# Regrouping the scores to three and five, one signed feature block per projection, and other places for 44 early units, in a two-branch attention kernel

## Chip, cores and metric

One core of one Trainium2 chip. The metric is the device time of one launch in microseconds (us); the time of a kernel is the median over its runs. Engines are named as in the profile: PE (TensorE), PEld (its weight loads), DVE (VectorE), ACT (ScalarE), POOL (GpSimd), SP (SyncE, which issues the DMAs).

## The reference

Inputs: x of 2048 tokens by 448, two sets of projection weights, a per-head feature matrix and a gate vector; 16 heads of 28.

```python
def _A_ref(x, wqkv, w_phi, wo):                   # linear attention with learned features
    q, k, v = ...                                 # x @ wqkv, by heads
    pq, pk = q @ w_phi, k @ w_phi                 # per head
    phi_q = concat([softmax(pq), softmax(-pq)])   # phi_k likewise from pk
    kv, z = phi_k^T v, sum(phi_k)
    return ((phi_q kv) / (phi_q z + 1e-6)) @ wo
def _B_ref(x, wqkv, wo):                          # full softmax attention
    return (softmax(q k^T * 28**-0.5) v) @ wo
g = sigmoid((x * gate_w).sum(-1))
return g * a + (1 - g) * b
```

The features of branch A need, for each head and token, the largest value and the smallest value of 28 numbers before two exponentials, exp(p - max) and exp(min - p).

## The kernel before, in words

The order of work on PE, DVE, ACT and POOL is the order of the Python calls (`manual_schedule`); only the DMAs on SP are placed by the framework. Times below are of the profiled execution.

**Projection of q and k of branch B** (to about 65 us): for n = 4 to 19 `proj_qk` (line 577) runs 11 matmuls into one PSUM bank, ACT and DVE split the result into a high and a low part (`keep_qk`, line 586) and SP writes it to DRAM. Weights are split in the same way by `split_weight` (line 141): a cast on ACT (line 143), a difference on DVE or POOL (line 144). `wvA` is split at n = 16 and 18 (line 688).

**Units** (`mx_unit`, line 259): the exact row maximum of the scores of branch B, which the softmax subtracts, costs a second pass over q k^T. In the early part it is done in 44 units: four matmuls on 28 rows side by side into two double banks `pmb` and `pmd` (line 285), a Relu of `pmd` on ACT (line 288), two add-and-max operations on DVE (line 290). There are two double-buffered banks for `pmb` and `pmd`, so a unit waits until DVE and ACT have read the one before. The units are sprinkled over the early loops by hand (lines 685, 733, 772, 818, and `tick`, line 719, inside a projection).

**Branch A** (about 65 to 316 us), the loop at line 727 over i = 0 to 42, with t = i for the keys (t < 16) and q = i - 16 for the queries. For each tile of 128 tokens `features1` (line 438) copies the projected block from PSUM to `pc` on ACT (line 441), takes maximum and minimum over each head on DVE (lines 443, 444), and makes the two differences (lines 447, 449: the first on POOL, the second on POOL or, for q = 1 to 8, on DVE). The exponential follows on ACT (line 452) one iteration later, and `features2` (line 455) sums on DVE, inverts, and multiplies on POOL (line 461). Features go to one of four buffers, `feats`. Keys end in `kv_add` (line 473); queries go through `turn` (transposes, copied to `fT` on ACT, line 528), `numer` (copied to `oUa` on ACT, line 399), a normalisation through DRAM, and `out_a` (line 557). At q = 2 the PSUM pool is closed and a new one opened with four single banks in place of three and the bank of `pkv`. From q = 18 the values of branch B are projected (`value_b`, line 712); `wvB` is split at q = 14 and 17.

**Branch B** (from about 332 us), the loop at line 1139 over s = 0 to 255. A step s is one tile of 128 keys against a block of 4 heads and 512 queries; 16 steps make a block, and there are 16 blocks. `scores` (line 879) does four matmuls `st` of 128x512 into four PSUM banks (line 885) and four exponentials on ACT (line 903); `values(s - 1)` does four column-tiled matmuls `pv` (line 1017) on the exponentials of the step before; `mx_visit` (line 305) carries on the row maxima: four row-tiled matmuls `pm` (line 322) into four more banks, one Relu or copy on ACT (line 326), two or three maxima on DVE (line 333) and mostly one add-and-max on DVE (line 330). PE thus runs st x4, pv, pm, st x4, and so on. Seven banks are dealt out from a list, `free`, by `scores` and `mx_banks` (line 956); an eighth holds the sum of `pv`. In the steady state the four banks of a step's `st` are, in order: the third and the fourth of the step before, the last one that DVE read of the `pm` of two steps before, and the one that ACT's Relu read of the `pm` just before. From s = 191 scores come in groups of eight, one for two steps, and a visit in every other step. `project` (line 1022) and the tail use the same list.

Of the kernel before, what the change touches and what calls it, by code (L numbers as in the profile page):

```python
# [17 lines left out]
P = 128  # L18
# [22 lines left out]
def gated_mix_kernel(ctx, tc, xT, wqkB, wvB, wvA, wkAT, wqAT, phi, woA, woB,  # L41
# [17 lines left out]

    psn = [3, 2]  # L60

    def ps_s(nm):
        return ps.tile([P, 512], F32, tag="s", name=nm, bufs=psn[0])

    def ps_pv(nm):
# [371 lines left out]

    def features1(pp, nm, eng):

        pc = bd.tile([P, H, DH], F32, tag="pc", name=f"pc{nm}", bufs=2)  # L440
        nc.scalar.copy(pc, pp[:, :D].rearrange("p (h f) -> p h f", f=DH))
        ext = bd.tile([P, 2, H], F32, tag="ext", name=f"ext{nm}", bufs=3)
        nc.vector.tensor_reduce(ext[:, 0, :], pc, AX.X, ALU.max)
        nc.vector.tensor_reduce(ext[:, 1, :], pc, AX.X, ALU.min)
        f = feats[feats_used[0] % 4]
        feats_used[0] += 1
        nc.gpsimd.tensor_sub(f[:, :, :DH], pc,
                             ext[:, 0, :].unsqueeze(2).to_broadcast([P, H, DH]))
        eng.tensor_sub(f[:, :, DH:2 * DH],
                       ext[:, 1, :].unsqueeze(2).to_broadcast([P, H, DH]), pc)  # L450
        fx = f[:, :, :2 * DH]
        exps.append(lambda: nc.scalar.activation(fx, fx, AF.Exp))
        return f
# [158 lines left out]
    def split_part(w, key, n, i, low=nc.vector):  # L612
        split_weight(w, raws[key][i], slice(2 * i, 2 * i + 2), slice(0, n), low)

    def splits(n):

# [47 lines left out]
    for n in range(4, NP):  # L664
        take_acts()
        if n in (4, 5):
            x_loads(n - 2)
        if n == 8:
            nc.sync.dma_start(phi_s, phi)
            load_fold(wkAT, "k")  # L670
        if n == 10:
            part_loads("wB1", wqkB[:, :, 512:896], 384, "wB1")
        splits(n + 1)
        if n == 14:
            part_loads("wvA", wvA, 450, "wvA")
            nc.sync.dma_start(sel_s, sel)
            nc.sync.dma_start(mask_s, mask)
            for v in vap:
                nc.gpsimd.memset(v[:, :, 28:32], 0.0)
                nc.gpsimd.memset(v[:, :, 28:29], 1.0)  # L680
            feats = [bd.tile([P, H, 64], F32, name=f"feat{i}") for i in range(4)]
            for f in feats:
                nc.gpsimd.memset(f[:, :, 56:], 0.0)
        if 16 <= n < 20:
            mx_unit()
        proj_qk(n, ev)
        if n in (16, 18):
# [39 lines left out]
    for i in range(2 * NT + 11):  # L727
# [14 lines left out]
        if q == 2:  # L742
            bk_s.close()
            ta_s = ExitStack()
            ta = ta_s.enter_context(tc.tile_pool(name="ta", bufs=1, reuse_waits="tile"))
            stg = ta_s.enter_context(tc.tile_pool(name="stg", bufs=2, reuse_waits="tile"))
            KV = ta.tile([P, 512], F32, name="KV")
            kvT = kv_copy()
            ps_s_.close()
            ps = ps_s_.enter_context(tc.tile_pool(name="psq", bufs=1, space=PSUM, reuse_waits="tile"))  # L750
            psn[0] = 4
            woA_s = weights(3, "woA_s")
            wvB_s = weights(2, "wvB_s")
            take_exps()
# [124 lines left out]
    def scores(s, i):  # L879
# [8 lines left out]
        if s == 0:  # L888
# [6 lines left out]
            return  # L895
        sts = []
        for j in (2 * i, 2 * i + 1):
            used.append(free.pop(0))
            sts.append(bank(used[-1], f"st{s}_{j}"))
            score(j, sts[-1])  # L900
        for j, st in enumerate(sts, 2 * i):
            p = p_slot(f"p{s}_{j}")
            nc.scalar.activation(p, st, AF.Exp, scale=SCALE)  # L903
            pts.setdefault(s, []).append(p)
        if i == 1:
            a, m = used[:], held[:]
            if s < TWO:
                free.extend([a[0], m[0], a[1], m[1], a[2], a[3], m[2]] if m else a)
            elif s % 2:
                free.extend([m[0], a[0], m[1], a[1]] if m else a)  # L910
                rest.extend([m[2], a[2], a[3]] if m else [])
            else:
                free.extend(rest + a)
                rest.clear()
            used.clear()
            held.clear()

    qst = [stack("qst0", False)]
    kst = [stack(f"kst{i}", True) for i in range(5)]
# [4 lines left out]
    ps_s_.close()  # L924
    ps = ps_s_.enter_context(tc.tile_pool(name="psv", bufs=1, space=PSUM, reuse_waits="tile"))
    psn[:] = 2, 3
    rlp = fr_s.enter_context(tc.tile_pool(name="rlp", bufs=1, reuse_waits="tile"))
    mx_unit()
    rest = NF - mxs["u"]
# [17 lines left out]

    free, used, held = list(range(7)), [], []  # L950
    spare, rest = [], []

    def bank(i, nm):
        return ps2.tile([P, 512], F32, tag=f"g{i}", name=nm, bufs=1)

    def mx_banks(f, first):
        b = [free.pop(0) for _ in range(4)]
        free.append(b[0])
        held.extend(b[1:])
# [62 lines left out]
    def project(qb, oT, tl):  # L1022
# [1 line left out]
        t = qb * 4 + tl  # L1024
        acc = acc_of[qb][:, tl, :]
        b = free.pop(0)
        free.append(held.pop(0) if held else b)
        if free[-1] != b:
            held.insert(0, b)
# [109 lines left out]
    for s in range(NS + 16):  # L1139
        take_acts()  # L1140
        if s < NS:
# [105 lines left out]
```

## Time and profile before

| | |
|---|---|
| time, median of 3 runs | 1017.42 us (1017.32 to 1019.32) |
| time of the profiled execution | 1015.89 us |
| its span on the core | 1014.1 us |
| instructions | 17989 |
| PE busy | 1002.8 us (99%) |
| ACT busy | 815.7 us (80%) |
| DVE busy | 679.7 us (67%) |
| POOL busy | 236.0 us (23%) |
| granted PE clock | 1.00 throughout |

The profile is of one execution. An engine is busy while one of its instructions runs; for PE the end of a matmul is modelled, and pipelined matmuls overlap, so that a PE that is busy all the time may still run under its best pace. Where an engine was idle before an instruction, the profile names the instruction that ended last among those it waited for. In the rows a time in us and a length in us stand first, then the engine, the line, the operation, the tile written and those read, the shape and a count of merged instructions; what stands in square brackets is the idle time before and what ended it.

### The profile page before, as it was taken

What the parts mean: (1) busy time and instruction counts of PE and PEld (TensorE: products, weight loads), DVE (VectorE), ACT (ScalarE), POOL (GpSimd) and SP (SyncE); (2) the same over time, 40 slices, a digit from 0 to 9 for tenths busy, and PEclk for the clock granted to TensorE, in tenths of its full rate; (3) what the DMA queues carried; (4) which work ended last, traced back from release to release, by engine and by line L of the source; (5) the groups of instructions that cost most, each with busy time, mean ns of one, the idle gap of its engine ahead of it and who ended that gap; (6) DMA issues with size and microseconds to landing.
All of it is one profiled execution on the core that took longest, in us unless ns stands there. A gap on an engine that the chain in (4) does not pass through costs nothing.

```text
span 1014.1 us, 17989 instructions
## 1 busy us (share of the span) xinstructions
PE 1002.8 (99%) x6472; PEld 561.9 (55%) x6472; DVE 679.7 (67%) x1340; ACT 815.7 (80%) x1534; POOL 236.0 (23%) x213
## 2 busy tenths in 40 slices
PE   9999999999999999999999999999999999999998
PEld 8878888868779433343333334333333344454656
DVE  6466666997753578888887888788888874544202
ACT  5445445678762899999999999999999999979682
POOL 1235456588435102111011110101201011001010
PEclk9999999999999999999999999999999999999999
DMA  8973110132245703233622223522323345615131
GB/s 295 311 241 93 60 50 3 44 90 83 93 129 128 155 20 84 64 73 69 128 65 70 55 58 79 127 65 55 87 56 76 75 101 155 157 34 150 57 109 55
DMA packets 64250, 98.89 MB, mean 98 GB/s; under 512 B 18176, under 2 KB 24944, under 8 KB 64160
## 3 DMA queue, kind: packets, MB, share of 16 engines
q1 hardware_dynamic: 64160, 97.74, 35.9%
q8 instruction: 51, 0.84, 0.4%
q14 instruction: 39, 0.32, 0.1%
HBM read 69.54 MB, written 27.78 MB: 96 GB/s over the span
## 4 chain that ended last, share of the span: by engine, by line
PE 90%; DVE 5%; DMA 2%; ACT 1%; POOL 1%; issue 1%; SPq 0%; DVEq 0%; POOLq 0%; ACTq 0%
PE st L885 29%; PE pv L1017 25%; PE pm L322 9%; PE pk L127 4%; PE pva L127 4%; PE poa L109 4%; PE pqk L109 3%; PE pob L109 3%; PE pvb L109 2%; PE pvb L127 2%; PE pq L109 2%; DMA qkd<-ev 1%; PE pmb L285 1%; PE pqk L652 1%; DVE fsumq L459 1%; DVE rl L290 1%
## 5 line engine op out<-in xcount | busy, mean ns | idle before, releaser
L903 ACT ACTIVATE p<-st 128x512 f32<-128x512 f32 x1020 | 522.4, 619 | 25.9 <-PE st L885 25.8
L333 DVE TENSOR_REDUCE part<-pm 128x1 f32<-128x512 f32 x477 | 304.6, 685 | 150.3 <-PE pm L322 144.3
L885 PE MATMUL st<-qst,kst 128*128 128x512 f32 x1024 | 309.8, 429 | 0.9 <-ACT vb L715 0.5
L1017 PE MATMUL pv<-p,vb 128*32 128x512 f32 x2048 | 266.1, 603 | 0.0
L885 PEld LDWEIGHTS st<-qst,kst 128*128 128x128 f32 x1024 | 174.2, 187 | 120.0 <-issue 52.4
L322 PEld LDWEIGHTS pm<-kc,qc 28*128 28x128 f32 x848 | 40.5, 181 | 177.8 <-ACT p L903 150.9
L326 ACT ACTIVATE rl<-pm 128x512 f32<-128x512 f32 x212 | 126.9, 598 | 10.8 <-PE pm L322 0.7
L420 POOL TENSOR_TENSOR oUb<-oUb,rsb 128x512 f32<-128x512 f32 x15 | 19.3, 1289 | 462.3 <-DMA rsb<-rdb 328.9
L330 DVE CUSTOM_DVE_ANT_0 rl<-pm,rl 128x512 f32<-128x512 f32 x159 | 108.1, 680 | 0.0
L322 PE MATMUL pm<-kc,qc 28*128 28x512 f32 x848 | 106.8, 495 | 0.0
L1017 PEld LDWEIGHTS pv<-p,vb 128*32 128x32 f32 x2048 | 45.5, 108 | 73.6 <-issue 67.4
L290 DVE CUSTOM_DVE_ANT_0 rl<-pmb,rl 128x512 f32<-128x512 f32 x88 | 57.0, 685 | 29.4 <-ACT rl L288 29.4
L109 PE MATMUL pqk<-XH,wB 128*128 128x512 f32 x192 | 59.3, 397 | 0.0
L288 ACT ACTIVATE rl<-pmd 128x1024 f32<-128x1024 f32 x44 | 45.2, 1028 | 12.0 <-PE pmd L285 5.6
L589 ACT CAST ev<-pqk 128x512 fp32r<-128x512 f32 x28 | 16.1, 588 | 35.2 <-PE pqk L109 24.9
L109 PE MATMUL poa<-woA_s,oTa 128*128 128x448 f32 x192 | 43.5, 374 | 0.2 <-POOL oTa L429 0.2
L109 PEld LDWEIGHTS pqk<-XH,wB 128*128 128x128 f32 x192 | 35.4, 188 | 8.5 <-issue 1.5
L1032 DVE SCALAR_TENSOR_TENSOR acc<-pob,gate,acc 128x448 f32<-128x448 f32 x12 | 8.2, 684 | 47.2 <-PE pob L109 47.2
L196 POOL TENSOR_TENSOR kc<-kc,kd 28x512 fp32r<-28x512 f32 x12 | 15.3, 1277 | 102.2 <-DMA kc<-qkd 85.7
L109 PEld LDWEIGHTS poa<-woA_s,oTa 128*128 128x128 f32 x192 | 34.9, 188 | 6.6 <-issue 3.3
L109 PE MATMUL pq<-wqA_s,XH 128*128 128x448 f32 x128 | 37.3, 374 | 0.8 <-DVE ev L590 0.8
L127 PE MATMUL pk<-wkA_s,XH 128*128 128x448 f32 x128 | 37.9, 377 | 0.0
(161 smaller groups left out, 1153.3 us busy)
## 6 DMA issues: line engine op xcount, KB each, us to landing
qkd<-ev SPq DMA_DIRECT2D x28, 512.0 KB
qst<-qkd SPq DMA_DIRECT2D x64, 224.0 KB
kst<-qkd SPq DMA_DIRECT2D x64, 224.0 KB
od<-oTb SPq DMA_DIRECT2D x48, 112.0 KB
rsa<-rda SPq DMA_DIRECT2D x8, 512.0 KB
rsb<-rdb SPq DMA_DIRECT2D x15, 256.0 KB
kc<-qkd SPq DMA_DIRECT2D x64, 56.0 KB
gad<-ga SPq DMA_DIRECT2D x16, 224.0 KB
```

Source lines behind the costliest of these rows:

```text
L109: nc.tensor.matmul(dst, l, r, start=i == 0, stop=i == len(todo) - 1)
L127: nc.tensor.matmul(dst[:, :n], l, r, start=i == 0, stop=i == len(todo) - 1, skip_group_check=True)
L288: nc.scalar.activation(rl, pd, AF.Relu)
L290: nc.vector.tensor_tensor_reduce(rl[:, i, :], pb[:, i, :], rl[:, i, :], 1.0, LOWEST, ALU.add, ALU.max, part[:, col + i:col + i + 1])
L322: nc.tensor.matmul(pm[j], mxs[("qc", gq)][js, qt * P:(qt + 1) * P], mxs[("kc", g, kb)][js, :], start=True, stop=True, tile_position=(32 * ...
L326: nc.scalar.activation(rl, pm[kb], AF.Relu if kb < 3 else AF.Copy)
L330: nc.vector.tensor_tensor_reduce(r, pm[j], r, 1.0, LOWEST, ALU.add, ALU.max, part[:, col + j:col + j + 1])
L333: nc.vector.tensor_reduce(part[:, col + j:col + j + 1], pm[j], AX.X, ALU.max)
L420: (nc.gpsimd if n == 1 else nc.vector).tensor_mul(oU, oU, rs)
L885: nc.tensor.matmul(st, kst_of[(g, kt // 4)][:, j, (kt % 4) * P:(kt % 4 + 1) * P], qst_of[gq][:, j, :], start=True, stop=True)
L903: nc.scalar.activation(p, st, AF.Exp, scale=SCALE)
L1017: nc.tensor.matmul(pv[32 * j:32 * j + 32, :], vb[kt // 8][:, kt % 8, 4 * g + j, :], pt[j], start=kt == 0, stop=kt == NT - 1, tile_position ...
```

## The change

Six edits:

1. `features1`: ACT writes the projected block twice into the feature buffer, as it is and times -1 (two reads of PSUM). One DVE maximum over 896 columns gives the maximum of both signs, and one difference over 896 columns takes the place of two. This difference is on DVE for q = 1, 3, 5 and 7 and on POOL for all others. `pc` is gone.
2. `wvA` is split by POOL alone (cast and difference), where ACT and DVE did it.
3. Units: three in place of two for t = 4, 6 and 8; none at q = 8, 9 and 10; one in place of two at q = 19 to 25. The last three of the 44 then run in the projection of branch B's values, after the PSUM pool is opened for it.
4. PSUM at q = 2 is no longer closed and reopened: every fourth single bank that is asked for is the one that held `pkv`, the other three rotate as before.
5. `wvB` is split at q = 13 and 15.
6. In the loop over s, odd steps put out three scores (heads 0 to 2 of s), even steps five (head 3 of s - 1, then all of s), up to s = 190. The list of banks is dealt out anew (`score_group`). From s = 191 the groups of eight and the order of their banks are as before. The first banks dealt are 0, 2 and 3.

In the steady state after the change the three scores of an odd step take the banks of the third, fourth and fifth score of the group before; the five of an even step take the bank of the second score of the group before, that of DVE's last read of the `pm` before, that of the third score, then that of the Relu of the `pm` just before and that of DVE's first read of it.

```diff
+    turn4 = []
     def ps_s(nm):
+        if turn4:
+            turn4.append(nm)
+            if len(turn4) % 4 == 0:
+                return ps_pv(nm)
         return ps.tile([P, 512], F32, tag="s", name=nm, bufs=psn[0])
...
-        pc = bd.tile([P, H, DH], F32, tag="pc", name=f"pc{nm}", bufs=2)
-        nc.scalar.copy(pc, pp[:, :D].rearrange("p (h f) -> p h f", f=DH))
-        ext = bd.tile([P, 2, H], F32, tag="ext", name=f"ext{nm}", bufs=3)
-        nc.vector.tensor_reduce(ext[:, 0, :], pc, AX.X, ALU.max)
-        nc.vector.tensor_reduce(ext[:, 1, :], pc, AX.X, ALU.min)
         f = feats[feats_used[0] % 4]
         feats_used[0] += 1
-        nc.gpsimd.tensor_sub(f[:, :, :DH], pc,
-                             ext[:, 0, :].unsqueeze(2).to_broadcast([P, H, DH]))
-        eng.tensor_sub(f[:, :, DH:2 * DH],
-                       ext[:, 1, :].unsqueeze(2).to_broadcast([P, H, DH]), pc)
+        f2 = f[:, :, :2 * DH].rearrange("p h (s f) -> p h s f", f=DH)
+        x = pp[:, :D].rearrange("p (h f) -> p h f", f=DH)
+        nc.scalar.copy(f2[:, :, 0, :], x)
+        nc.scalar.mul(f2[:, :, 1, :], x, -1.0)
+        ext = bd.tile([P, H, 2], F32, tag="ext", name=f"ext{nm}", bufs=3)
+        nc.vector.tensor_reduce(ext, f2, AX.X, ALU.max)
+        eng.tensor_sub(f2, f2, ext.unsqueeze(3).to_broadcast([P, H, 2, DH]))
...
-            split_part(wvA_s, "wvA", 450, (n - 16) // 2)
+            split_part(wvA_s, "wvA", 450, (n - 16) // 2, nc.gpsimd, nc.gpsimd.tensor_copy)
...
-            pace["n"], pace["at"] = 4 if t >= 4 else 0, [passes // 2]
+            pace["n"] = 4 if t >= 4 else 0
+            pace["at"] = [passes // 3, 2 * passes // 3] if t in (4, 6, 8) else [passes // 2]
...
-            ps_s_.close()
-            ps = ps_s_.enter_context(tc.tile_pool(name="psq", bufs=1, space=PSUM, reuse_waits="tile"))
-            psn[0] = 4
+            turn4.append("")
...
-            fq[q] = features1(pq, f"q{q}", nc.vector if 0 < q < 9 else nc.gpsimd)
+            fq[q] = features1(pq, f"q{q}", nc.vector if q in (1, 3, 5, 7) else nc.gpsimd)
...
-        if q in (0, 1) or q >= 8:
+        if q in (0, 1) or q >= 11:
             mx_unit()
...
-        if q in (14, 17):
-            split_part(wvB_s, "wvB", D, (q - 14) // 3)
+        if q in (13, 15):
+            split_part(wvB_s, "wvB", D, (q - 13) // 2)
...
-        if NT + 3 <= q < NT + 10:
-            mx_unit()
...
+    def score_group(sc):
+        n, take = len(sc), []
...
+        elif n == 3:
+            free.extend(last)
+            last.clear()
+            u = pop(3)
+            free.extend([mb[0], mb[1], u[0], mb[2], u[1], mb[3], u[2]])
+        elif n == 5:
+            free.extend(mb[:2])
+            u = pop(5)
+            free.extend([u[0], mb[2], u[1], mb[3], u[2]])
+            last.extend(u[3:])
...
-            for z in ([s] if s < TWO else [s, s + 1][:NS - s] if s % 2 else []):
-                if z:
-                    scores(z, 0)
-                    scores(z, 1)
+            if s and s < TWO:
+                score_group([(s, j) for j in range(3)] if s % 2
+                            else [(s - 1, 3)] + [(s, j) for j in range(4)])
+            elif s % 2:
+                score_group([(z, j) for z in (s, s + 1) if z < NS for j in range(4)])
```

More of the change, by code (lines that the diff above doesn't have):

```diff
@@ L610, in part_loads, with split_part @@
         loads(key, lambda: load_part(src, n, nm, 0), lambda: load_part(src, n, nm, 2))
-    def split_part(w, key, n, i, low=nc.vector):
-        split_weight(w, raws[key][i], slice(2 * i, 2 * i + 2), slice(0, n), low)
+    def split_part(w, key, n, i, low=nc.vector, high=nc.scalar.copy):
+        split_weight(w, raws[key][i], slice(2 * i, 2 * i + 2), slice(0, n), low, high)
     def splits(n):
@@ L894, in scores, with pop @@
             pts.setdefault(s, []).extend([p[:, 0, :], p[:, 1, :]])
[L895 to L901, printed above, removed]
+    def score_group(sc):
+        n, take = len(sc), []
+        def pop(k):
+            got = [free.pop(0) for _ in range(k)]
+            take.extend(got)
+            return got
+        if not mb or n == 4:
+            free.extend(last)
+            last.clear()
+            pop(min(n, 4))
+            free.extend(take)
+            if n == 8:
+                u = pop(4)
+                free.extend(u)
+        elif n == 3:
+            free.extend(last)
+            last.clear()
+            u = pop(3)
[5 more added lines that the diff above has]
+            last.extend(u[3:])
+        else:
+            free.extend(last + mb[:1])
+            last.clear()
+            u = pop(4)
+            free.extend([mb[1], u[0], mb[2], u[1]])
+            v = pop(4)
+            free.extend([mb[3], u[2], u[3]] + v)
+        mb.clear()
+        for (s, j), i in zip(sc, take):
+            gq, kt = divmod(s, NT)
+            st = bank(i, f"st{s}_{j}")
+            nc.tensor.matmul(st, kst_of[(gq // NQ, kt // 4)][:, j, (kt % 4) * P:(kt % 4 + 1) * P],
+                             qst_of[gq][:, j, :], start=True, stop=True)
             p = p_slot(f"p{s}_{j}")
@@ L904, in scores @@
             pts.setdefault(s, []).append(p)
[L905 to L916, printed above, removed]
     qst = [stack("qst0", False)]
@@ L926, in gated_mix_kernel @@
     psn[:] = 2, 3
+    turn4.clear()
     rlp = fr_s.enter_context(tc.tile_pool(name="rlp", bufs=1, reuse_waits="tile"))
@@ L946, in gated_mix_kernel @@
     ps2 = ctx.enter_context(tc.tile_pool(name="ps2", bufs=1, space=PSUM, reuse_waits="tile"))
-    free, used, held = list(range(7)), [], []
-    spare, rest = [], []
+    free, mb, last, spare = [0, 2, 3, 4, 5, 1, 6], [], [], []
     def bank(i, nm):
@@ L957, in mx_banks @@
         b = [free.pop(0) for _ in range(4)]
-        free.append(b[0])
-        held.extend(b[1:])
+        mb.extend(b)
         order = [first] + sorted({0, 1, 2, 3} - {first}, key=lambda j: j == first - 1)
@@ L1026, in project @@
         b = free.pop(0)
-        free.append(held.pop(0) if held else b)
-        if free[-1] != b:
-            held.insert(0, b)
+        free.append(mb.pop(0) if mb else b)
+        if mb:
+            mb.insert(1, b)
         po = bank(b, f"pob{t}")
```

## The prediction

> **What bounds the kernel now.** I read the busy time by stage first, then PE's idle times, then the two steady patterns instruction by instruction. Stages, in us of the span (busy time and count for PE, PEld, DVE, ACT, POOL; then granted clock, DMA share, GB/s):
>
> ```profile
> 0.00:64.60 64.60, 61.61 (x289) 49.56 (x289) 38.08 (x61) 32.14 (x46) 12.24 (x27) 1.00 0.89 298
> 64.60:177.00 112.40, 112.40 (x984) 94.34 (x985) 69.90 (x146) 54.73 (x92) 63.04 (x54) 1.00 0.22 66
> 177.00:224.00 47.00, 44.08 (x413) 35.12 (x411) 43.52 (x80) 34.09 (x56) 31.87 (x24) 1.00 0.23 64
> 224.00:316.00 92.00, 91.22 (x600) 73.48 (x593) 56.24 (x122) 61.27 (x97) 49.20 (x38) 1.00 0.31 98
> 335.00:830.00 495.00, 494.77 (x3035) 193.56 (x3035) 397.92 (x802) 484.63 (x949) 52.40 (x50) 1.00 0.34 78
> ```
>
> The key part of branch A (64.6 to 177) is PE alone: never idle, others at half. The first query iterations (177 to 224) have DVE at 93% and PE idle for 2.9 us. The long loop (335 to 830, 190 steps) has PE and ACT both near full, so there one has to see which of them waits. PE's idle times outside the loop that the change touches:
>
> ```profile
> 56.49 0.50 PE L285 MATMUL pmd<-kp,qp 28*128 28x512 f32 x2 [0.92 <-DVE part L290]
> ...
> 64.09 0.50 PE L285 MATMUL pmd<-kp,qp 28*128 28x512 f32 x2 [0.71 <-DVE part L290]
> ...
> 184.39 0.67 PE L109 MATMUL pq<-wqA_s,XH 128*128 128x448 f32 x2 [0.81 <-DVE ev L590]
> ...
> 213.80 0.50 PE L285 MATMUL pmd<-kp,qp 28*128 28x512 f32 x2 [2.10 <-DVE part L290]
> ...
> 259.83 0.50 PE L285 MATMUL pmd<-kp,qp 28*128 28x512 f32 x2 [0.58 <-DVE part L290]
> ...
> 335.23 0.96 PE L885 MATMUL st<-qst,kst 128*128 128x512 f32 x3 [0.48 <-ACT vb L715]
> ```
>
> Four of the six are a unit that waits until DVE has read the unit before. Now one step of the loop, under the page's row of all its exponentials:
>
> ```profile
> L903 ACT ACTIVATE p<-st 128x512 f32<-128x512 f32 x1020 | 522.4, 619 | 25.9 <-PE st L885 25.8
> ...
> 538.03 0.50 PE L322 MATMUL pm<-kc,qc 28*128 28x512 f32 x4
> 538.46 0.53 PEld L885 LDWEIGHTS st<-qst,kst 128*128 128x128 f32 x3 [0.24 <-issue]
> 538.47 1.24 PE L885 MATMUL st<-qst,kst 128*128 128x512 f32 x4
> 538.56 0.60 ACT L326 ACTIVATE rl<-pm 128x512 f32<-128x512 f32 x1
> 538.60 1.29 DVE L333 TENSOR_REDUCE part<-pm 128x1 f32<-128x512 f32 x2
> 539.06 2.06 ACT L903 ACTIVATE p<-st 128x512 f32<-128x512 f32 x4
> 539.21 0.19 PEld L885 LDWEIGHTS st<-qst,kst 128*128 128x128 f32 x1 [0.22 <-ACT rl L326]
> 539.64 0.16 PEld L1017 LDWEIGHTS pv<-p,vb 128*32 128x32 f32 x8 [0.24 <-issue]
> ...
> 540.63 0.19 PEld L322 LDWEIGHTS pm<-kc,qc 28*128 28x128 f32 x4 [0.84 <-ACT p L903]
> ```
>
> The step is 540.63 - 538.03 = 2.60 us. ACT takes five operations in it, at (2.06 - 0.62)/3 = 0.48 us from one to the next (0.62: the mean of one), 2.4 us: ACT has 0.2 us to spare and is not the bound. PE is, and one thing in its chain is a wait: the fourth score's weight load starts only when the Relu has ended (538.56 + 0.60 = 539.16) and 0.05 us have gone by, 0.4 us after the third load started, because the fourth score takes the Relu's bank.
>
> **The change, part by part.** The sum is made against the profiled execution's 1015.89 us (span 1014.1, 1.8 around it); the median of the three runs shown, 1017.42, is 1.53 above it, and I put the forecast at that level.
>
> *Scores in threes and fives, 95 pairs of steps.* No instruction comes or goes. In an odd step none of the three scores takes a bank of the `pm` just before, so its wait goes; the even step keeps the same wait at its fourth score. What is one wait worth? Groups of eight scores that wait for nothing, late in the trace:
>
> ```profile
> 953.28 1.76 PEld L885 LDWEIGHTS st<-qst,kst 128*128 128x128 f32 x8
> ...
> 963.37 2.14 PE L885 MATMUL st<-qst,kst 128*128 128x512 f32 x8
> 965.44 1.92 PE L1017 MATMUL pv<-p,vb 128*32 128x512 f32 x16
> 967.29 2.11 PE L885 MATMUL st<-qst,kst 128*128 128x512 f32 x8
> 969.33 0.16 PEld L1017 LDWEIGHTS pv<-p,vb 128*32 128x32 f32 x8 [0.35 <-issue]
> ```
>
> From first score to first value product they take 2.07 and 2.04 us. By the loads a score in a stream costs (1.76 - 0.19)/7 = 0.22, so four fewer would take 1.14 to 1.17. The waiting group takes 539.64 - 538.47 = 1.17: by this a wait costs 0 to 0.03. By the load alone it costs up to 0.18: the third load starts at 538.46 + 0.53 - 0.19 = 538.80, the fourth was due at 539.02 and came at 539.21. I take 0.05, near the first figure, since a group's length holds what really reaches the value products, and a little above it, since the two late groups had no maximum pass and began at another pace. 95 x 0.05 = **4.8** gained (0 to 17).
>
> Do new waits appear? From the step above, shifted by one score: in the even step the fifth score's load is due at 539.21 + 0.22 = 539.43, and its bank is free when DVE's first read ends, 538.60 + 0.69 (a single read) + 0.05 = 539.34: 0.09 to spare. The first of the five must be exponentiated before `pv`, 539.06 + 0.62 + 0.05 = 539.73 against 539.64 + 0.23 = 539.87: 0.14 to spare. The fifth exponential starts at 539.06 + 4 x 0.48 = 540.98 and ends at 541.60; its bank is the third one of the next odd step, whose load is due 0.77 after that step's `pm` (538.03 to the third load, 538.80, is 0.77), at 540.63 + 0.23 + 0.77 = 541.63 against 541.65: on the edge, and I count nothing. Over a pair ACT needs ten times 0.48 against 5.15.
>
> *`wvA` on POOL.* Off ACT and DVE go these:
>
> ```profile
> 53.14 0.95 ACT L143 CAST wvA_s<-wvA_raw 128x900 fp32r<-128x900 f32 x1 [0.60 <-DMA wvA_raw<-in_wvA_dram]
> ...
> 54.12 1.09 DVE L144 TENSOR_TENSOR wvA_s<-wvA_raw,wvA_s 128x900 fp32r<-128x900 f32 x1 [0.86 <-ACT wvA_s L143]
> ...
> 59.13 2.64 POOL L221 TENSOR_TENSOR kp<-kp,kt 28x512 fp32r<-28x512 f32 x2 [11.27 <-DMA kt<-qkd]
> ...
> L144 POOL TENSOR_TENSOR woB_s<-woB_raw,woB_s 128x448 fp32r<-128x448 f32 x4 | 4.6, 1146 | 0.3
> ...
> L143 POOL CAST woB_s<-woB_raw 128x448 fp32r<-128x448 f32 x4 | 2.2, 557 | 10.4 <-DMA woB_raw<-in_woB_dram 10.4
> ```
>
> They stand right ahead of the Relu and the DVE reads for which PE then waits 0.92 and 0.71, so up to 1.63 goes. On POOL, scaled by 900/448, a part costs 1.12 + 2.30; two from 53.14 end at 59.98. Behind them on POOL is the difference of `kp` (59.13, 2.64 long), now done at 62.6; the fifth unit needs it and comes at 64.09 - 0.71 - 0.50 = 62.88, less 0.92, so 62.0. So some 0.6 is given back: **1.0** (0.3 to 1.6).
>
> *PSUM at q = 2.* The new pool's first bank waits for a late read of an old one, 0.81. In the rotation that `pq` takes a bank read long before: **0.8** (0 to 0.8).
>
> *Units.* Each costs PE the same anywhere; what goes is the wait of those at q = 8 to 10, where DVE is full. The three put into the key part find DVE at 62%, the three put last an idle DVE, and there and at q = 19 to 25 a unit's price on PE only changes place. Their loads of `kc`, `qc` and `qp` move with them on SP; those for the second head group fall behind the key stacks, which costs nothing as they are due some 20 steps into the loop. **2.1** (0 to 2.1).
>
> *Features.* In the query iterations before the output products start:
>
> ```profile
> L441 ACT COPY pcq<-pq 128x448 f32<-128x448 f32 x6 | 3.2, 536 | 5.1 <-PE pq L109 5.1
> ...
> L449 DVE TENSOR_TENSOR feat<-extq,pcq 128x448 f32<-128x448 f32 x6 | 6.0, 1002 | 0.6
> L459 DVE TENSOR_REDUCE fsumq<-feat 128x32 f32<-128x896 f32 x5 | 5.4, 1075 | 0.1
> L444 DVE TENSOR_REDUCE extq<-pcq 128x16 f32<-128x448 f32 x6 | 3.6, 607 | 0.0
> L443 DVE TENSOR_REDUCE extq<-pcq 128x16 f32<-128x448 f32 x6 | 3.5, 590 | 1.1 <-ACT pcq L441 1.0
> ...
> 195.06 1.23 DVE L449 TENSOR_TENSOR feat<-extq,pcq 128x448 f32<-128x448 f32 x1
> ...
> 194.11 1.71 POOL L461 TENSOR_TENSOR feat<-feat,fsumq 128x896 f32<-128x896 f32 x1 [2.61 <-DVE fsumq L460]
> ```
>
> DVE: one maximum over 896 (price of the 896-column sum, 1.08) for 0.59 + 0.61, and no difference in even iterations, so some 4 us fewer over q = 1 to 8. That pays only by the waits named already. ACT: one more read of PSUM per tile, about 0.5. In the key part it lies beside PE's work (ACT at 49%). In these six iterations ACT's only real idle time is the 5.1 it waits for `pq`, against 6 x 0.5 = 3.2 added, and behind the new instruction on ACT stand the copies that free PSUM for PE (`fT`, `oUa`). I charge **1.0** (0 to 4.5, all of it in q = 2 to 10). The copy now waits for the transposes of the tile four back, which PE ended an iteration before.
>
> The DVE difference above ran 1.23, over the group's mean of 1.00, and ended 0.47 after POOL's product had (194.11 + 1.71 = 195.82): it stood still while POOL worked. [...]
>
> *`wvB` earlier* takes its DVE difference away from the unit at 259.83: **0.4** of 0.58. *First banks 0, 2, 3*: the scores of s = 1 no longer wait for the copy of the last value tile: **0.5**.
>
> Sum: 4.8 + 1.0 + 0.8 + 2.1 - 1.0 + 0.4 + 0.5 = 8.6. So 1007.3 for a profiled execution, **1008.8** at the median's level.
>
> **Rivals.**
>
> *A. The loop gains nothing* (the third score of the odd step waits for the fifth exponential instead; by the figures above it is 0.02 late already): 1017.42 - 3.8 = 1013.6. [...]
>
> *B. Both waits of a pair go* because the five-group leaves the Relu time, and ACT's extra work is hidden: 9.5 for 4.8 and no 1.0, 5.7 more: 1003.1. Against it: `pm`, Relu and fourth score stand as before.
>
> *C. Slower: the five-group's last score waits for DVE.* A late DVE can be seen in the groups of eight:
>
> ```profile
> 835.16 2.50 PE L885 MATMUL st<-qst,kst 128*128 128x512 f32 x8
> ...
> 839.88 2.21 PE L885 MATMUL st<-qst,kst 128*128 128x512 f32 x8
> ```
>
> 0.29 more; 0.2 in each pair is 19: 1027.8. It turns the sign from 8.6/95 = 0.09 per pair on. Against it: 0.09 to spare, and DVE is at 80% in the loop.
>
> *D. ACT becomes the bound of the query part*: 14 iterations of 0.40 (0.54 less the 0.14 by which ACT's instructions overlap: four of 0.62 take 2.06), 5.6 for 1.0: 1013.4. For it: little idle time at q = 4 to 10. Against it: from q = 11 the output products come on top for PE, twelve matmuls an iteration.
>
> **Numbers.** Forecast 0.52, A 0.16, B 0.10, C 0.08, D 0.10, A and D together (1018.2) 0.04. About 0.2%, 2 us, is what a measurement can tell from no change. Faster: 0.52 + 0.16 + 0.10 + 0.10 = 0.88; same 0.04; slower 0.08. The range, 1002.0 to 1014.5, takes in A, B and D with the bounds of the smaller terms; it leaves out C, A with D, and the upper end of the loop's term (996), to which I give a part of the forecast's 0.52, some 0.05.
>
> **What would show it.** A pair of steps of 5.16 instead of 5.22, the load of the odd step's third score with no idle time, that of the fourth of five still ended by the Relu. No idle PE over 0.3 us at 55 to 65 and 183 to 223. The loop's start earlier by 4 to 5 us. I am wrong if PE's loads in the loop wait for an exponential or for DVE, or if PE in the query part waits for ACT's copies.

## The result, and the profile after

The changed kernel takes **1010.75 us** in the median of six runs (1008.13 to 1012.57), the kernel before 1017.37 (1016.89 to 1019.32): a ratio of 0.9931 with a 95% interval of 0.9914 to 0.9948, or 6.6 us less, where 8.6 were forecast. The profiled execution took 1011.92 with a span of 1010.1, against 1015.89 and 1014.1. Its runs differ more than those of the kernel before, and their mean granted clocks differ with them: 1.000 in the run of 1008.13, 0.998 in those of 1009.24 and 1009.86, 0.997 in the other three (1011.63 to 1012.57).

First the changed kernel's stages, with the columns of the prediction's table:

```profile
0.00:64.60 64.60, 63.24 (x295) 51.45 (x296) 37.63 (x60) 31.51 (x45) 18.47 (x31) 1.00 0.87 298
...
177.00:224.00 47.00, 42.88 (x396) 34.63 (x402) 40.73 (x56) 35.07 (x63) 29.39 (x19) 0.98 0.21 63
224.00:316.00 92.00, 91.58 (x605) 73.94 (x586) 49.46 (x105) 60.31 (x100) 46.86 (x32) 0.97 0.29 90
...
335.00:830.00 495.00, 495.00 (x3065) 190.74 (x3067) 400.45 (x806) 479.92 (x959) 53.79 (x51) 1.00 0.36 80
```

Up to 64.6 PE is idle for 1.36 us instead of 2.99: the waits at 56 and 64 are gone. In the loop PE issues 3065 matmuls in the same 495 us instead of 3035. But from 177 to 224, where 2.9 us of waits were to vanish, PE is idle for 4.1, and there and up to 316 the granted clock, 1.00 everywhere in the profile before, is 0.98 and 0.97.

The loop, in the timeline of one pair of steps:

```profile
539.12 0.51 PE L328 MATMUL pm<-kc,qc 28*128 28x512 f32 x4
...
539.55 0.53 PEld L935 LDWEIGHTS st<-qst,kst 128*128 128x128 f32 x3 [0.25 <-ACT p L938]
...
539.64 0.60 ACT L332 ACTIVATE rl<-pm 128x512 f32<-128x512 f32 x1 [0.15 <-PE pm L328]
...
540.29 0.32 PEld L935 LDWEIGHTS st<-qst,kst 128*128 128x128 f32 x2 [0.21 <-ACT rl L332]
...
541.95 0.50 PE L328 MATMUL pm<-kc,qc 28*128 28x512 f32 x4
...
542.38 0.54 PEld L935 LDWEIGHTS st<-qst,kst 128*128 128x128 f32 x3 [0.24 <-ACT p L938]
...
544.28 0.51 PE L328 MATMUL pm<-kc,qc 28*128 28x512 f32 x4
```

The pair takes 544.28 - 539.12 = 5.16 us, 2.83 with five scores and 2.33 with three. The fourth of the five still waits for the Relu (540.29, 0.21); the three loads at 542.38 run through without a break. It is so in the whole loop: from 338 to 830 the profile puts 189 idle times of PEld ahead of a score down to the Relu in the kernel before (41.7 us in all), 96 in the changed one (20.8), and none to DVE. Over the whole loop and what follows it, the first and the last `pm` stand here in the kernel before, and then in the changed one (the third column's range is first and last start):

```profile
L322 PE MATMUL pm<-kc,qc x848: 489/497/502, 337.1 to 937.7; 28*128 28x512 f32 x170
```

```profile
L328 PE MATMUL pm<-kc,qc x848: 488/497/502, 337.6 to 933.8; 28*128 28x512 f32 x170
```

That is 600.6 and 596.2 us: **4.4 gained in the loop**. The loop begins 0.5 later, so the front as a whole gained nothing in this execution. PE's waits in the query part and up to 316 (in all, times, longest) say why:

```profile
PE pn L543 <- ACT fT L532: 3.1, 1, 3.1
PE pft L529 <- DVE KV L517: 0.8, 1, 0.8
PE pmd L291 <- DVE part L296: 0.4, 1, 0.4
```

The wait of 3.1 us, followed back through the timeline:

```profile
209.27 0.53 SPq L420 DMA_DIRECT2D rsa<-rda  x1
...
217.59 1.71 POOL L465 TENSOR_TENSOR feat<-feat,fsumq 128x896 f32<-128x896 f32 x1
...
218.06 2.32 DVE L426 TENSOR_TENSOR oUa<-oUa,rsa 128x1024 f32<-128x1024 f32 x1 [1.00 <-DMA rsa<-rda]
...
220.42 1.14 ACT L434 CAST oTa<-oUa 128x512 fp32r<-128x512 f32 x2 [3.28 <-DVE oUa L426]
...
222.31 1.05 ACT L532 COPY fT<-pft 128x512 f32<-128x512 f32 x2
...
222.93 1.96 PE L543 MATMUL pn<-fT,KV 56*32 56x256 f32 x32 [3.14 <-ACT fT L532]
224.82 4.63 PE L115 MATMUL poa<-woA_s,oTa 128*128 128x448 f32 x12
```

Read it from the top. The reciprocals of the first block of queries, spread over the partitions (`rsa`, 512 KB), are issued at 209.27; DVE's multiplication by them can start at 218.06 only, and with POOL at work beside it, it takes 2.32 where it takes 1.16 undisturbed. ACT's cast of the product stands in ACT's queue ahead of the copies of `fT`, and waits 3.28 for it. PE needs `fT`. In the kernel before the chain ends at the same time, but there PE has no wait at `pn`: it comes there some 3 us later.

```profile
208.89 0.53 SPq L414 DMA_DIRECT2D rsa<-rda  x1
...
219.07 1.16 DVE L420 TENSOR_TENSOR oUa<-oUa,rsa 128x1024 f32<-128x1024 f32 x1
...
222.98 1.09 PE L539 MATMUL pn<-fT,KV 56*32 56x256 f32 x32
```

In the changed kernel DVE ended 1.08 us after POOL (220.38 against 217.59 + 1.71 = 219.30), about the length of an undisturbed multiplication (1.16): by that it stood still while POOL worked. It is so in all the differences that DVE makes for the features: the eight over 448 columns in the kernel before end 0.47 to 0.49 after the POOL instruction beside them, the four over 896 in the changed kernel 0.95 after it. The prediction's sum has no term for that; at the multiplication it is some 1.2 us (2.32 - 1.16), at a place where the end of the chain hangs on it.

Behind the wait PE is slow: `pn` took 1.96 (1.09 before), twelve `poa` 4.63 (2.7 elsewhere). The windows show the clock (the last but two of the columns):

```profile
218.83:222.24 3.41, 0.96 (x7) 0.34 (x5) 2.55 (x2) 1.82 (x3) 1.19 (x2) 1.00 0.11 26
222.24:225.65 3.41, 2.72 (x34) 1.41 (x35) 3.14 (x5) 2.92 (x6) 3.41 (x3) 0.50 0.26 103
225.65:229.07 3.42, 3.42 (x10) 3.02 (x10) 2.67 (x7) 1.93 (x3) 3.37 (x3) 0.50 0.17 41
```

For 6.83 us the clock is half. So my theory after the result: the front's gain on PE was real, and was lost to a chain from DMA over DVE and ACT that did not move with PE, and to the half clock that followed the wait.

### The profile page after: what moved, and what is told of

Its sections match the earlier page's. It is cut to its first block, busy times and chain, and to the rows that moved or that the text cites. A ratio compares the mean times of both kernels' runs of the same rounds, so it can differ in the third digit from the quotient of the medians.

```text
span 1010.1 us, 17959 instructions
## 1 busy us (share of the span) xinstructions
PE 1000.1 (99%) x6472; PEld 557.3 (55%) x6472; DVE 674.2 (67%) x1302; ACT 816.2 (81%) x1564; POOL 234.6 (23%) x189
## 4 chain that ended last, share of the span: by engine, by line
PE 76%; DMA 1%; ACT 1%; DVE 1%; issue 0%; ACTq 0%
PE st L935 28%; PE pv L1039 25%; PE pm L328 9%; PE poa L115 4%; PE pob L115 3%; PE pvb L133 2%; PE pvb L115 2%; PE pq L115 1%; DMA dena<-oUa 1%; PE poL L1077 1%; PE pmb L291 1%; PE pft L529 0%; PE pn L543 0%; PE poL L1147 0%; ACT feat L456 0%; DVE part L339 0%
## 5 line engine op out<-in xcount | busy, mean ns | idle before, releaser
L938 ACT ACTIVATE p<-st 128x512 f32<-128x512 f32 x1020 | 529.3, 639 | 25.7 <-PE st L935 25.7
L935 PE MATMUL st<-qst,kst 128*128 128x512 f32 x1020 | 303.2, 423 | 0.3 <-DVE acc L1054 0.3
L935 PEld LDWEIGHTS st<-qst,kst 128*128 128x128 f32 x1020 | 167.9, 187 | 99.2 <-ACT p L938 48.6
L332 ACT ACTIVATE rl<-pm 128x512 f32<-128x512 f32 x212 | 132.2, 624 | 15.5 <-PE pm L328 13.7
L454 POOL TENSOR_TENSOR feat<-feat,extk 128x896 f32<-128x896 f32 x16 | 27.3, 1705 | 56.2 <-DVE extk L453 42.4
L133 PE MATMUL pva<-wvA_s,XH 128*128 128x450 f32 x128 | 37.6, 371 | 0.0
```

The source lines that it names most:

```text
L133: nc.tensor.matmul(dst[:, :n], l, r, start=i == 0, stop=i == len(todo) - 1, skip_group_check=True)
L332: nc.scalar.activation(rl, pm[kb], AF.Relu if kb < 3 else AF.Copy)
L454: eng.tensor_sub(f2, f2, ext.unsqueeze(3).to_broadcast([P, H, 2, DH]))
L935: nc.tensor.matmul(st, kst_of[(gq // NQ, kt // 4)][:, j, (kt % 4) * P:(kt % 4 + 1) * P], qst_of[gq][:, j, :], start=True, stop=True)
```

## Experiments

All times are medians; each ratio is to the kernel before as it was timed beside the experiment (1017.22 for `e1` to `e4`, 1016.77 for `e5` to `e8`, 1017.48 for `e9` to `e12`), with its 95% interval.

**1. The two halves alone.** `e1_loop` is the kernel before with `score_group`, its bank lists and the first banks; `e2_front` is the changed kernel with the old `scores` and bank lists.

> The kernel before with the regrouped loop alone (threes and fives, first banks 0, 2, 3); the whole front is the old one. Theory: a pair of steps costs 0.058 us less, as the two traces show (5.218 to 5.16), 95 pairs give 5.5, so 1011.9, with a clock that stays full and runs that lie within 1 us of each other. Rival (the loop's gain is partly eaten at its ends or by the exponentials): 1013.5 to 1017.4.

> The changed kernel with the old loop (fours) and so the front edits alone. Theory: the front edits gain about 4 us early and lose a PE wait of 3 us plus some 3.4 us of half clock at 223, so the median is within 1.5 us of before, 1016 to 1017, and the runs spread over 4 us with the granted clock: 1013.5 when the clock stays full, 1018 when it halves. Rival (the front is worth nothing and has no part in the spread): 1017.4 with a spread of 0.5.

`e1_loop` took 1013.02 (1011.84 to 1014.04), ratio 0.9957 (0.9945 to 0.9970), 4.2 less by the medians and 4.4 by the ratio. Its `pm` run from 339.2 to 935.4, 596.2 us as in the changed kernel. `e2_front` took 1014.99 in eleven runs (1013.53 to 1017.25), ratio 0.9979 (0.9970 to 0.9988), 2.2 less. The two add up to 6.4 by the medians, the measured whole being 6.6. The loop's gain is nearer 4.4 than 5.5: the whole loop counts, not one pair. The front is worth a little more than I had thought, and its runs do spread over 3.7 us, though none had a full clock. What I had not expected is that the runs of `e1_loop` spread over 2.2, and that it halved its clock too, with the old front, for 3.41 us from 214.57, behind the old wait at the unit:

```profile
213.81 0.50 PE L291 MATMUL pmd<-kp,qp 28*128 28x512 f32 x2 [2.13 <-DVE part L296]
```

Nor is this the regrouping's doing: of the 33 runs of the kernel before that were timed beside the experiments, 27 have a mean clock of 0.997 or 0.998. So by its mean clock it too has some half clock in most of its runs, and the profile before, at 1.00 throughout, is the less common case. Where its clock fell no trace shows, and its runs at full clock (1015.59 to 1017.62) are hardly shorter than the others (1016.02 to 1019.13).

**2. The wait, and the clock behind it.** `e4_fill` gives PE something to do in the wait:

```diff
+        for i in range(10 if tb == 3 else 0):
+            nc.tensor.matmul(pn[0][:, :P], ident, ident, start=True, stop=True)
         for gp in range(2):
```

> The changed kernel with ten more matrix products of the identity, about 2.4 us at full clock, into the bank of the numerator just before PE's 3.14 us wait; their result is overwritten. Nothing is due earlier or later for it. Theory: the wait stays, but PE is no longer idle for long, so the granted clock stays full and the time is that of the changed kernel's full clock run, 1008.1 to 1008.5, in every run. Rival (the half clock costs nothing, because the output products that follow wait for their operands anyway): 1010.7 as it stands, with the same spread.

It took 1009.01 (1008.54 to 1009.81), ratio 0.9920 (0.9907 to 0.9934), with a mean clock of 1.000 in all five runs:

```profile
218.56 2.50 PE L539 MATMUL pn<-ident 128*128 128x128 f32 x20
221.77 1.16 PE L545 MATMUL pn<-fT,KV 56*32 56x256 f32 x32 [0.72 <-ACT fT L532]
222.86 2.44 PE L115 MATMUL poa<-woA_s,oTa 128*128 128x448 f32 x10
```

`pn` still comes 3.2 us after PE was free, but it and `poa` run at full speed. Work that computes nothing makes the kernel 1.7 us faster by the medians (the intervals of the two ratios overlap), and the runs lie within 1.3 us of each other where the changed kernel's spread over 4.4. It is half a us above what I had expected. With the changed kernel's own runs (1008.13 at full clock, 1011.63 to 1012.57 at 0.997) it points to a price of the half clock behind this wait, beside the wait itself.

**3. Two ways to shorten the wait.** `e3_early_norm` moves `normalize2` from the end of the iteration to its start, so that `rsa` is issued earlier. Three kernels put back units that the change had moved to the key part:

```diff
-pace["at"] = [passes // 3, 2 * passes // 3] if t in (4, 6, 8) else [passes // 2]
+pace["at"] = [passes // 3, 2 * passes // 3] if t in (4, 6) else [passes // 2]
-        if q in (0, 1) or q >= 11:
+        if q in (0, 1) or q >= 10:
```

This is `e5_one_unit`; `e6_two_units` has t = 4 alone and q >= 9, `e7_three_units` no t and q >= 8.

> The changed kernel; of the query part's normalisation only the step that takes the reciprocal and issues the two transfers stands earlier, at the start of its iteration instead of its end (some 2.4 us earlier on DVE). Theory: the 3.14 us wait of PE at 222.9 comes from that transfer by way of DVE's multiplication and ACT's queue, so it shrinks to under 1 us, the clock stays full, and the time is 1005 to 1006, with little spread. Rival 1 (the wait only moves, since the stage is DVE's): 1008 at full clock, 1010.7 if the clock still halves. Rival 2 (the transfer is not the cause): 1010.7 unchanged.

> The changed kernel with one of the three units put back from the key part to q = 10, ahead of PE's wait at 222.9 (two units stay in the key part). Theory: the end of that wait is set by the transfer of the reciprocals and DVE, not by PE, so a unit there costs PE nothing and the key part is 0.9 us shorter: the wait goes from 3.14 to about 2.2, the half clock becomes rare, 1007.2 to 1008.5. Rival (the step on record: a unit out of the query part is a gain): 1011 to 1011.5, as the unit's reads push DVE's chain back.

> The changed kernel with two of the three units put back, to q = 9 and q = 10. Theory: the wait at 222.9 falls to 1 to 1.5 us, but the second unit now waits for DVE's reads of the first, as in the kernel before (2.10 there): no more gain than with one unit, 1007 to 1008.5, little spread. Rival (the step on record): 1012 to 1012.5.

> The changed kernel with all three units back at q = 8, 9 and 10 (none extra in the key part). Theory: the wait at 222.9 is gone, the 2.10 wait at the second unit is back, and the full clock stays: 1007.5 to 1009. Rival (the step on record: 2.1 was gained by moving them): 1010.2 at full clock, 1012.9 at the level of the median.

`e3_early_norm` took 1023.76, ratio 1.0062 (1.0049 to 1.0074): 13 us worse than the changed kernel, against both rivals and the theory. Its timeline:

```profile
206.81 0.56 SPq L420 DMA_DIRECT2D rsa<-rda  x1
207.46 1.15 SPq L408 DMA_DIRECT2D dena<-oUa  x2
...
217.14 0.18 DVE L414 TENSOR_SCALAR dena<-dena 128x32 f32<-128x32 f32 x1 [5.33 <-DMA dena<-oUa]
...
222.21 1.97 PE L529 MATMUL pft<-ident,feat 128*128 128x128 f32 x8 [5.47 <-POOL feat L465]
```

`rsa` did start 2.5 us earlier. But SP now issued the next block's sums (`dena`, two transfers of 8 KB) right behind its 512 KB instead of ahead of it, and DVE had them 9 to 10 us after their issue. DVE stood for 5.33 us, with the features behind it in its order. The same comes again one block later: DVE stands for 4.76 us before 229.65, and PE for 4.77 before 234.29.

The units gave 1008.38 with one (1007.09 to 1010.20; ratio 0.9920, 0.9907 to 0.9934), 1011.10 with two (1009.66 to 1012.04; 0.9944, 0.9931 to 0.9956), and **1006.94** with three (1006.75 to 1009.98; 0.9912, 0.9899 to 0.9926). One unit came out at the time expected, but not as thought: its second half takes over most of the wait, and the half clock is not rare, with 6.83 us in the profile and a mean clock under 1.000 in three of the four runs.

```profile
221.21 0.79 PE L291 MATMUL pmd<-kp,qp 28*128 28x512 f32 x2 [2.51 <-DVE part L296]
```

Two units missed. The wait at `pn` is gone there, but the order of the two transfers has turned over as in `e3_early_norm`:

```profile
218.21 0.54 SPq L420 DMA_DIRECT2D rsa<-rda  x1
218.84 0.54 SPq L408 DMA_DIRECT2D dena<-oUa  x1
...
227.40 0.18 DVE L414 TENSOR_SCALAR dena<-dena 128x32 f32<-128x32 f32 x1 [6.29 <-DMA dena<-oUa]
...
230.17 0.51 PE L291 MATMUL pmd<-kp,qp 28*128 28x512 f32 x2 [2.29 <-DVE part L296]
```

Three units did better than I had thought:

```profile
210.70 0.50 PE L291 MATMUL pmd<-kp,qp 28*128 28x512 f32 x2 [0.67 <-DVE part L296]
...
214.19 1.16 SPq L408 DMA_DIRECT2D dena<-oUa  x2
...
215.91 1.16 DVE L426 TENSOR_TENSOR oUa<-oUa,rsa 128x1024 f32<-128x1024 f32 x1
...
217.39 0.53 SPq L420 DMA_DIRECT2D rsa<-rda  x1
```

The multiplication waits for nothing, the small transfer is ahead of the large one, PE has no wait at `pn`, and the unit that waited 2.10 before waits 0.67. So moving the units out of the query part was not the gain of 2.1 but, by every measure, a loss: 3.8 by the medians (1010.75 to 1006.94), 1.9 by the ratios (0.9931 to 0.9912, with intervals that overlap), 5.5 by the spans of the profiled executions (1010.1 to 1004.6), of which one has 6.83 us of half clock and the other none. At a mean clock of 1.000 the changed kernel has one run, 1008.13, and `e7_three_units` two, 1006.75 and 1007.08; the kernel before was 0.6 faster beside the latter. So the sign is likely and the size open. It is not PE's load alone that decides (two units are worse than one), but where PE's order meets the chain of transfers.

**4. The other front edits.** `e8_features` is the changed kernel with the old `features1`; the other three start from `e7_three_units`: `e10_old_features` has the old `features1`, `e11_old_wva` the old split of `wvA`, `e12_old_psum` the old second pool at q = 2.

> The changed kernel with the features as they were: one copy by ScalarE, a maximum and a minimum over 448 columns and two differences. All else as changed. The step on record charged the new features 1.0 (0 to 4.5), which would give 1009.7. Theory now: the stretch up to 223 waits for a transfer and for DVE, and the old features keep DVE busier by some 4 us there; so the old ones are no better, 1010.5 to 1012, the 3.14 us wait is as long or longer, and the clock halves as often.

> The kernel with the three units put back, and the features as they were in the kernel before. Theory: the new features are a gain there, since they leave DVE room for the units' reads (PE's wait at the unit of q = 9 is 0.67 with them, 2.10 in the kernel before); with the old ones that wait is back at about 2, and the clock may halve behind it: 1008.3, up to 1010 with half clock. Rival (the step on record, by which the new features cost 1.0): 1005.9.

> The kernel with the three units put back, and the split of wvA on ScalarE and VectorE again. Theory: the move is worth 2.2, since the key part's first matmul stands at 62.0 to 63.1 in the profiles with it and at 64.5 in the two without it: 1009.1. Rival (the step on record, by which 0.6 of 1.6 is given back): 1007.9.

> The kernel with the three units put back, and the second PSUM pool opened at q = 2 as before, in place of the rotation over four banks. Theory: the rotation took 0.8 away at q = 2 and put 0.79 back at the transposes of q = 4, so the old pool is no worse: 1006.9. Rival (the step on record, 0.8 gained and kept): 1007.7.

*Features.* `e8_features` took 1009.38 (1009.00 to 1010.63; ratio 0.9932, 0.9919 to 0.9944): 1.4 less by the medians, the same by the ratios, nearer the step on record than my new theory. Nor is the 3.14 us wait as long or longer there: PE has no wait at `pn`, and stands for 2.32 us at the transposes at 216.48 instead, until POOL's product of features is done. `e10_old_features` took 1008.43 (1006.81 to 1009.63; 0.9908, 0.9895 to 0.9922), 1.5 more than with the new features, though the ratios do not tell them apart. The profiles do: PE's wait at the second unit, 0.67 in `e7_three_units`, is back, and the clock is half for 6.83 us behind it.

```profile
210.95 0.75 PE L291 MATMUL pmd<-kp,qp 28*128 28x512 f32 x2 [2.00 <-DVE part L296]
```

The new features thus shorten that unit's wait by 1.3 where the units stay. A gain in time is not shown: at a mean clock of 1.000 `e10_old_features` took 1006.81 and 1006.92, `e7_three_units` 1006.75 and 1007.08.

*`wvA`.* `e11_old_wva` took 1007.73 (1007.19 to 1008.21; 0.9906, 0.9893 to 0.9922), 0.8 more by the medians and nothing by the ratios; the spans of the two profiles, both at full clock up to the last few microseconds, are 1006.3 and 1004.6. The two waits are there again, each about half as long as before (`e1_loop`, with the same code there as the kernel before, has 0.42 and 0.68, so their length differs from execution to execution):

```profile
57.03 0.50 PE L291 MATMUL pmd<-kp,qp 28*128 28x512 f32 x2 [0.39 <-DVE part L296]
...
64.25 0.50 PE L291 MATMUL pmd<-kp,qp 28*128 28x512 f32 x2 [0.34 <-DVE part L296]
```

My 2.2 was too much; 1.0 lies within what the runs can tell (nothing by the ratios, 0.8 by the medians, 1.7 by the spans).

*PSUM at q = 2.* `e12_old_psum` took 1011.57 (1009.03 to 1012.98; 0.9941, 0.9928 to 0.9954), 4.6 more by the medians and 2.9 by the ratios, whose intervals are apart: above either expectation.

```profile
179.42 1.82 DVE L454 TENSOR_TENSOR feat<-feat,extq 128x896 f32<-128x896 f32 x1
...
180.14 0.99 PE L483 MATMUL pkv<-feat,vap 128*32 128x56 f32 x64
...
183.12 0.67 PE L115 MATMUL pq<-wqA_s,XH 128*128 128x448 f32 x2 [1.98 <-DVE ev L594]
```

The old pool's wait, 0.81 in the kernel before, is 1.98 here. PE ends `pkv` at 181.1, 2.4 earlier than before (183.6), but the read that frees the bank ends only 1.3 earlier (183.06 against 184.34), with a difference over 896 columns ahead of it on DVE. Behind it a unit waits 1.30 and the clock halves for 3.41 us. The profiled execution is the fastest of the five; what the other four lost besides is not seen, though their mean clocks of 0.996 and 0.997 point to more half clock.

**5. A version that beats both.** `e9_kv_first` adds one move to `e7_three_units`:

```diff
+        if q == 3:
+            kv_out(kvT)
         if 0 <= q < NT:
             fq[q] = features1(pq, f"q{q}", nc.vector if q in (1, 3, 5, 7) else nc.gpsimd)
...
-        if q == 3:
-            kv_out(kvT)
```

> The kernel with the three units put back; also the turned sums of keys and values (kv_out, once, at q = 3) are issued ahead of that iteration's features instead of behind them, so that DVE copies them out of PSUM before the features' maximum and difference. Theory: PE's wait of 0.79 at the transposes of q = 4 is for that copy, whose bank they take in the new rotation; it goes, and the time is 0.8 less, 1006.1. Rival (the wait only moves behind the maximum that the copy pushes back, or comes back further on): 1006.9 as it was.

It took **1006.40** (1006.12 to 1009.86), ratio 0.9901 (0.9887 to 0.9915), 11.1 below the kernel before by the medians and 10.1 by the ratio. DVE's copy ran 3 us earlier (186.66) and the wait of 0.79 fell to 0.16, but `pn` then waited 0.51:

```profile
186.66 0.69 DVE L517 COPY KV<-pkvT 128x512 f32<-128x512 f32 x1 [0.39 <-PE pkvT L516]
...
190.35 0.66 PE L529 MATMUL pft<-ident,feat 128*128 128x128 f32 x4 [0.16 <-ACT fT L532]
193.87 1.15 PE L543 MATMUL pn<-fT,KV 56*32 56x256 f32 x32 [0.51 <-ACT fT L532]
```

The spans differ by 0.6 (1004.6 and 1004.0): most of the rival's "it comes back further on" is true. Against `e7_three_units` the gain is within what the runs can tell.

## Why the prediction was right, and where it was not

- *The loop, 4.8:* right, in size and place. `e1_loop` gained 4.2 by the medians, and in it and in the changed kernel the `pm` take 4.4 less from first to last, 0.046 per pair for 0.05. The lower of the two bounds, from the length of whole groups, was the right one to lean on; the load's 0.18 does not reach the end of a step. Rivals A, B and C fall with it: there is a gain, it goes with one Relu wait of two (189 to 96), and no score's load from 338 to 830 waits for DVE.
- *First banks, 0.5:* the wait of 0.48 at the loop's start is gone in the changed kernel, but `e1_loop`, which has the new first banks, still shows it at 337.6. So it is some front edit that took it away; which one was not tried.
- *`wvA`, 1.0:* right in place, the waits at 56 and 64 are gone; in size as far as the runs can tell (0.8 by the medians, 1.7 by the spans, nothing by the ratios).
- *PSUM, 0.8 with 0.8 as its upper bound:* the bound failed. It priced the old wait as it stood in the kernel before; with PE earlier and a longer DVE instruction the same pool would have cost 1.98 there. Of that, 0.80 came back at the transposes of q = 4 (193.18), whose bank is one that the rotation hands on from the turned sums. With the old features (`e8_features`, `e10_old_features`) or the old pool (`e12_old_psum`) this wait isn't there, so it takes both edits.
- *Units, 2.1:* the step that failed, and by all that was measured with the wrong sign. The prediction had it that "each costs PE the same anywhere; what goes is the wait of those at q = 8 to 10". The units at q = 8 to 10 also kept PE busy while a chain that PE does not set (`rsa`, multiplication, cast, `fT`) came to its end; without them PE came there early and stood for 3.14 us, and `pn` began at 222.93 where it had begun at 222.98. The row that would have told was in the profile before: that multiplication, at 219.07, stood only some 10 us behind the issue of its `rsa`, and the working never asked when the transfer landed.
- *Features, -1.0:* the charge was put on ACT. ACT was not short of time in the changed kernel (it waited 3.28 in the chain above), so rival D did not come about. What the new features are worth in time stays open (1.4 lost by the medians in `e8_features`, 1.5 gained in `e10_old_features`, nothing by the ratios of either). The sum has no term for the time that DVE stands still beside POOL, and at the differences it was small: DVE's four over 896 columns took 1.45 on average and 1.14 at the quickest, some 1.2 in all.
- *`wvB`, 0.4:* 0.36 of waiting is left at the unit at 267, of 0.58 at 260: about 0.2; but in `e7_three_units`, which has the early split too, it is 0.59, so no gain is shown.
- *The signs I had named:* 5.16, the third load and the Relu came as written. In the rows an exponential is named ahead of a group's first load (539.55, 0.25), but the idle time is that of the kernel before (538.46, 0.24), so no new wait is in it. No idle PE over 0.3 us at 55 to 65 came true, at 183 to 223 it did not, nor an earlier start of the loop, and "PE in the query part waits for ACT's copies" did happen. The total came within the range because the loop carried it and the front's errors, a loss at the units and a larger gain at the pool, partly cancelled. That part of the hit is luck: the front as a whole was put at 3.8 and gave 2.2.

## What to carry to other kernels

Before work is moved off an engine at a place where it seems to wait, ask what else ends there: follow the next wait of that engine back to its DMA, and see by how much that chain would move. If it doesn't move, the freed time turns into another wait, and on PE a wait may cost more than its length (here one of 3.14 us had 6.83 at half clock behind it, and work put into it made the kernel 1.7 faster by the medians). Where a small transfer that an engine's next instruction needs and a large one are issued on one queue (here 8 KB behind 512 KB, read 9 to 10 us after their issue), see to it that the small one goes first, and check this again after every edit that shifts either.

## What the runs showed of the hardware

*The clock.* In the nine profiles that have a halving inside the program, it lasts 3.41 us (as in `e1_loop`, `e6_two_units` and `e12_old_psum`) or twice that, 6.83 (as in the changed kernel, `e5_one_unit` and `e10_old_features`). Cut into windows of 3.41 that end where the clock falls, the last window before held between 1.30 and 3.41 us of idle PE. The least is that of `e12_old_psum`, whose window of 3.41 has 2.11 of PE:

```profile
209.43:212.84 3.41, 2.11 (x25) 1.15 (x31) 3.41 (x7) 2.13 (x6) 3.41 (x2) 1.00 0.42 132
212.84:216.25 3.41, 3.41 (x41) 2.44 (x26) 3.12 (x10) 2.86 (x5) 2.88 (x3) 0.50 0.59 145
```

The same profile's wait of 1.98 (181.14 to 183.12) fell half into one window of that phase and half into the next (about 1.0 of idle PE in each), and no halving stands behind it. But the idle time in a window doesn't seem to decide alone. In the changed kernel the clock falls at 222.24 and again, after PE's last work, at 1010.72: 788.48 us apart, 231 times 3.4133. If windows can be counted back so in the kernel before, from its fall at 1015.29, the window from 209.74 has 1.46 us of idle PE, most of the wait of 2.10, and no halving behind it:

```profile
209.74:213.16 3.42, 1.96 (x10) 1.25 (x8) 3.32 (x7) 1.70 (x4) 3.42 (x2) 1.00 0.35 106
213.16:216.57 3.41, 2.77 (x44) 1.98 (x45) 3.34 (x9) 2.18 (x4) 1.46 (x2) 1.00 0.65 169
```

Near its end it has 1.47 in the window from 1008.46 (1.94 of PE in 3.41), still at full clock in the next.

So 1.30 of 3.41 us of idle PE stood before a halving in one case, and, counted so, 1.46 and 1.47 did not in two others: these profiles give no fixed bound, and why some runs of one kernel halve the clock and some don't is not shown. How long a halving lasts goes mostly with its own first window: in the five with 0.64 us or more of idle PE there (0.69 in the changed kernel, 222.24 to 225.65) it lasted 6.83, in four of the five with none (`e12_old_psum` among them, 212.84 to 216.25) 3.41; the fifth, in `e10_old_features`, lasted 6.83 and stays unexplained. Nor is a lower mean clock always a longer time: `e8_features` took 1009.00 to 1009.38 in three runs at 0.997 and 0.998, 1010.40 and 1010.63 in two at 0.999.

*A transfer behind a large one.* Two transfers of 8 KB, issued right behind one of 512 KB from the same queue, reached DVE 9 to 10 us later (issued at 207.46 and 208.06, read at 217.14), in a case where DVE would have taken them by 211.8; in `e6_two_units` a single one took 8.6 (218.84 to 227.40). Issued ahead of the large one in the changed kernel, at 207.90 and 208.56, the pair was read at 213.39 without a wait. That it is the large transfer that holds them up is inferred from the order.
